# Attention outputs: their transposes ahead of a half run of values, their sums inverted by GpSimd

## The chip, the cores and the metric

One core of a Trainium2 chip runs the whole kernel. The metric is device time in microseconds (us) from launch to end, the median of several runs. The core's engines run in parallel, each in the order of its own queue, and wait for each other by semaphores: TensorE (PE in the profile, its weight loads PEld), VectorE (DVE), ScalarE (ACT), GpSimd (POOL), and SyncE (SP), which only issues transfers here. GpSimd issues transfers too.

## The reference

The kernel computes a conditioned transformer block on 2048 rows of 576 columns: layer norm and modulation, attention with 32 heads of 18 columns, then layer norm and a gated product. Only attention matters here; for each head it is

```python
H = 32; Dh = D // H            # D = 576, Dh = 18
scores = jnp.einsum("bhqd,bhkd->bhqk", q, k) * Dh ** -0.5
p = _softmax(scores, axis=-1)
o = jnp.einsum("bhqk,bhkd->bhqd", p, v)
x = x + ga * (o.transpose(0, 2, 1, 3).reshape(B, S, D) @ wo)
```

All data is in 32-bit floating point.

## The kernel before

**Units and steps.** Attention runs in 32 units (`u`): 16 pairs of heads (`p`) for the first 1024 query rows (`half` 0), then the same pairs for the other 1024. A unit has 16 steps (`kt`), one for each 128 keys. In a step TensorE makes four score tiles of 128 keys x 512 queries (L1055, two heads by two blocks of columns, each reading half of the array's rows), and ACT turns each into probabilities with one exponential (L1059). TensorE multiplies the probabilities of a step with the values two steps later (`values`, L629): four results side by side in one bank of PSUM, `o`, which gathers the sum over all 16 steps. A head's values have a 19th column of ones, so that row 18 of each head's result is the sum of the probabilities, by which the result has to be divided.

**Maxima.** The exponentials need each query's largest score. TensorE makes these scores ahead of time, for a later unit, with queries in rows (L524), and VectorE takes the maxima (L530, L535; for one tile in eight ACT helps with L533). The negated maxima of a unit are turned around (`spread`, L555) and stored as two more rows of the query operand.

**The order by hand.** In this stage the orders of TensorE and of ACT are written out; VectorE's and GpSimd's instructions are ordered by a planner when the kernel is built. A step's order is a string (L1028), one letter for each piece: `m` a score tile for maxima, `t` a score tile with its exponential, `v` a whole run of values (512 columns), `a` and `b` the two half runs (256 columns each) of another step's values, `k` the copy of a finished `o` (`taken`), `w` or `s` the place where outputs, `spread` and background work issue their first part, `c` where outputs and `spread` issue their second part.

There are two forms. The "halved" one has `vmmtmmtsactt` in even steps and `wmcmbkttmtmt` in odd ones. The other, for steps with much background work, has `vtmmttmvtm` and `ktmwttmctmm`. The form is chosen at each even step (L1021 to L1025), from step 10 on by

```python
hold = heavy and (kt == 2 or kt == 12 and u < UNITS - 1)
state["halved"] = step >= 10 and (hold or not heavy)
```

so steps 2 and 3 of every later unit are halved.

**Outputs.** When a unit's 16 runs of values are done, in step 1 of the next unit, ACT copies `o` to SBUF as `oT` (`taken`, L646). `outputs` (from L649) then has two parts. The first issues four transposes of 128x128 on TensorE (L656) into one PSUM bank, `tp`, which puts queries in rows. The second, at `c`, has VectorE take the reciprocal of the 16 sums per row from `tp` (L661, 128x16), ACT copy `tp` back over `oT` (L672, 128x512), and GpSimd multiply each head's 144 values with the reciprocals into the rows `Oa` or `big` (L676, two of 128x144). For the very last unit, both the reciprocal and the products are VectorE's (L665). In the kernel before, `outputs` is called in step 3 at `w`, so the transposes stand at the head of step 3, between two score tiles of step 2 and a tile for maxima.

**Banks.** Scores, maxima and transposes take turns in seven PSUM banks (`bank`, L89): each tile waits until the tile seven before it in this order has been read.

**Background work.** From unit 15 on, `first_rows` and `last_rows_project` project finished rows of outputs, one piece at a time, at the same letters: transposes L743 and L760, products L776, and in units 22 to 25 the transposes L886 of the normalized rows `z`, which GpSimd makes (L866). Earlier, `weigh` (L114) and `down_parts` (L912 on) use GpSimd to prepare weights of the next stage.

Of the kernel before, what the change touches and what calls it, by code (L numbers as in the profile page):

```python
# [15 lines left out]
F32 = mybir.dt.float32  # L16
F32R = mybir.dt.float32r
AF = mybir.ActivationFunctionType
ALU = mybir.AluOpType
# [4 lines left out]
P = 128  # L24
# [4 lines left out]
DH = 18  # L29
# [32 lines left out]
def tile_block(ctx, tc, x_in, wqkv, wo, w_gate, w_up, w_down, c_in, w_mod, out):  # L62
    nc = tc.nc
# [3 lines left out]
    const = ctx.enter_context(tc.tile_pool(name="const", bufs=1))  # L67
# [6 lines left out]
    make_identity(nc, ident)  # L74
    powers = const.tile([P, 8], F32, name="powers")
    nc.gpsimd.memset(powers, -0.5)
    mcol = const.tile([P, 2, 5], F32, name="mcol")
    mcol2 = const.tile([P, 2, 6], F32, name="mcol2")
    gb_b = const.tile([P, D], F32, name="gb_b")
    left = ExitStack()  # L80
# [8 lines left out]
    def bank():  # L89

        turns["bank"] += 1
        return ps[turns["bank"] % 7].tile([P, 512], F32, name=f"s{turns['bank'] % 7}")
# [458 lines left out]
    def spread(qs, nm):  # L551

        n = HW // P
        tp = bank()[0 : 2 * n, 0:P]
        nc.tensor.transpose(tp, nm.rearrange("p h t -> p (h t)"), ident)  # L555
        yield
        mrows = small.tile([32 + 2 * n, P], F32R, name="mrows", bufs=1)
        parts = [mrows[32 * l : 32 * l + 2 * n] for l in range(2)]
        nc.scalar.copy(parts[0], tp)
        nc.vector.tensor_sub(parts[1], tp, parts[0].bitcast(F32))  # L560
        for h in range(2):
            for l, part in enumerate(parts):
                to = 64 * h + 3 * DH + l
                nc.sync.dma_start(
                    qs[to : to + 1, :].rearrange("l (t q) -> l t q", q=P).bitcast(F32),
                    part[n * h : n * (h + 1), :].bitcast(F32),
                )
# [4 lines left out]
    def turn():  # L572
        if turns["s"] < turns["to"]:
            turns["s"] += 1
            next(todo, None)
# [37 lines left out]
    epool = att.enter_context(tc.tile_pool(name="epool", bufs=1))  # L613
# [6 lines left out]
    def values(cols=slice(0, 512)):  # L620

        half, p, kt, probs = pending[0]
        if kt == 0:
            state["o"] = po.tile([P, 512], F32, name="o")
        acc = state["o"]
        for h in range(2):
            for c in range(2):
                j = 2 * h + c
                nc.tensor.matmul(  # L629
                    acc[32 * j : 32 * j + 32, cols],  # L630
                    vaug[:, kt, (2 * p + h) * VW : (2 * p + h) * VW + 32],
                    probs[2 * c + h][:, cols],
                    start=kt == 0, stop=kt == NT - 1 and cols.stop == 512, tile_position=(0, 32 * j),
                )
        if cols.stop < 512:
            return
        pending.pop(0)
        if kt == NT - 1:
            state["whole"] = (half, p, acc)

    def taken():

        if "whole" in state:
            half, p, acc = state.pop("whole")
            oT = epool.tile([P, 512], F32, name="oT")
            nc.scalar.copy(oT, acc)  # L646
            state["end"] = (half, p, oT)

    def outputs():  # L649

        if "end" not in state:
            return
        half, p, oT = state.pop("end")
        tp = bank().rearrange("p (b q) -> p b q", q=P)
        for b in range(4):
            nc.tensor.transpose(tp[:, b, :], oT[:, b * P : (b + 1) * P], ident)  # L656

        yield
        tq = tp.rearrange("p b (j e) -> p j b e", e=32)
        rec = epool.tile([P, 4, 4], F32, name="rec")  # L660
        nc.vector.reciprocal(rec, tq[:, :, :, DH])  # L661
        if half == 1 and p == H // 2 - 1:
            state["last"] = epool.tile([P, 512], F32, name="oT")[:, 0 : 16 * DH].rearrange("p (t e) -> p t e", t=8)
            for h in range(2):
                nc.vector.tensor_tensor(  # L665
                    state["last"][:, :, h * DH : (h + 1) * DH].rearrange("p (c b) e -> p c b e", c=2),
                    tq[:, 2 * h : 2 * h + 2, :, 0:DH],
                    rec[:, 2 * h : 2 * h + 2, :].unsqueeze(3).to_broadcast([P, 2, 4, DH]),
                    op=ALU.mult,
                )  # L670
            return
        nc.scalar.copy(oT, tp.rearrange("p b q -> p (b q)"))  # L672
        tq = oT.rearrange("p (b j e) -> p j b e", j=4, e=32)
        for h in range(2):
            f0 = (2 * p + h) * DH
            nc.gpsimd.tensor_tensor(  # L676
                Os[half][:, :, f0 : f0 + DH].rearrange("p (c b) e -> p c b e", c=2),
                tq[:, 2 * h : 2 * h + 2, :, 0:DH],
                rec[:, 2 * h : 2 * h + 2, :].unsqueeze(3).to_broadcast([P, 2, 4, DH]),
                op=ALU.mult,  # L680
            )
# [328 lines left out]
    for u in range(UNITS):  # L1010
        half, p = divmod(u, H // 2)
# [5 lines left out]
        for kt in range(NT):  # L1017
# [11 lines left out]
            for does in order[kt % 2]:  # L1029
                if does == "m":  # L1030
                    turn()
                elif does == "k":
                    taken()
                elif does in "ws":
                    if kt == 3:
                        follow.append(outputs())
                        next(follow[-1], None)
                    if "spread" in state and halved == (does == "s"):
                        follow.append(spread(*state.pop("spread")))
                        next(follow[-1])  # L1040
                    if step >= FROM0 and not hold and halved == (does == "s"):
                        state["next"] = next(rows0 if step < FROM1 else rows1, None)
                elif does == "c":
                    while follow:
                        next(follow.pop(0), None)
                elif does == "v":
                    if step >= LAG:
                        values()
                elif does in "ab":
                    values(slice(0, 256) if does == "a" else slice(256, 512))  # L1050
                else:
                    c, h = next(sides)
                    sT = bank()
                    rows = slice(64 * h, 64 * h + 3 * DH + 2)
                    nc.tensor.matmul(  # L1055
                        sT, ks[rows, kcols], qs[rows, c * 512 : (c + 1) * 512], start=True, stop=True
                    )
                    pr = probs[2 * c + h] = ppool.tile([P, 512], F32, name=f"p{2 * c + h}")
                    state["exp"] = nc.scalar.activation(pr, sT, AF.Exp, scale=SCALE)  # L1059
            pending.append((half, p, kt, probs))  # L1060
            if u in (1, 3):
                if kt == 0:
                    a = big.tile([P, 8, 640], F32, name="big")
                    a = a.rearrange("p a b -> p (a b)")[:, 0 : 8 * D].rearrange("p (t c) -> p t c", t=4)
                    b = slots.tile([P, 2560], F32, name="w0")[:, 0 : 2 * D]
# [39 lines left out]
    for _ in outputs():  # L1105
        pass
# [13 lines left out]
    def region(name):  # L1120
        return ctx.enter_context(tc.tile_pool(name=name, bufs=1))
# [6 lines left out]
    sums = {1: region("sums"), 3: region("sums3")}  # L1128
# [456 lines left out]
    for n, (hf, b, k) in enumerate(seq):  # L1585
# [167 lines left out]
        if hf == 0 and b == NB - 1:  # L1753
# [3 lines left out]
            s = ORDER.index(k)  # L1757
# [31 lines left out]
```

## Time and profile before

| | us |
|---|---|
| runs shown (3): median | 2802.2 |
| lowest, highest | 2801.63, 2802.61 |
| span of the profiled execution, first to last instruction | 2801.3 |
| first and last L656 start | 280.5, 1536.0 |
| L656: 128 matmuls, median of one | 0.273 |
| L661: 32 reciprocals, median of one | 0.257 |
| L672: 31 copies by ACT, median of one | 0.736 |
| L676: 32 and 30 products by GpSimd, median of one | 0.432 and 0.430 |

The profiled execution's own time isn't given apart from its span; the median of the runs is 0.9 us above that span. TensorE's granted clock was 0.999 of full speed over the span.

In the timeline's rows the columns are: start, duration (of all instructions in the row, from the first start to the last end), engine, line, operation, tiles written and read, shape, and how many instructions the row merges. Square brackets give idle time of that engine before the row and what ended it. A weight load (PEld) marks the point at which TensorE takes up the matmul that belongs to it. In rows by line, the last columns are the total busy time in us, the mean of one in ns, and idle time before them in us.

### The profile page before, as it was taken

Reading aid. Unit: us, or ns where it says so; the run is one execution under the profiler, and the core shown is the slowest. Engines: PE = TensorE matmul, PEld = TensorE weight load, DVE = VectorE, ACT = ScalarE, POOL = GpSimd, SP = SyncE. Lnnn points to the kernel's source line nnn. Section 1 sums busy time; section 2 is a strip of 40 time slices with the busy share of each in tenths; the row PEclk is TensorE's granted clock in tenths of the full one; section 3 lists DMA queues with packets and bytes.
Section 4 is the critical chain, followed back from the end, with each engine's and each line's share of the span. In section 5 each row is a group of like instructions: output and inputs, shape, how many; then the busy total and the mean of one; then the engine's idle time right before and its main releaser. Section 6 shows DMA issues by size and latency. Waiting matters only on the chain.

```text
span 2801.3 us, 50850 instructions
## 1 busy us (share of the span) xinstructions
PE 2766.6 (99%) x18637; PEld 1830.4 (65%) x18637; DVE 2302.7 (82%) x4370; ACT 1607.0 (57%) x3051; POOL 816.2 (29%) x1077
## 2 busy tenths in 40 slices
PE   7999999999999999999999999999999999999999
PEld 5975444444444444444444888888888888888888
DVE  7278999999998888999883788888898677777777
ACT  3216999999999778999888322333333222222221
POOL 3125208887843111663113222222221100000000
PEclk9999999999999999999999999999999999999999
DMA  5344215444442120232126766667767966666663
GB/s 173 123 155 147 72 59 173 168 173 157 170 135 80 36 59 24 98 106 71 43 68 219 266 220 228 232 217 266 279 249 274 355 201 196 203 196 200 199 197 120
DMA packets 170778, 462.60 MB, mean 165 GB/s; under 512 B 21212, under 2 KB 88032, under 8 KB 160416
## 3 DMA queue, kind: packets, MB, share of 16 engines
q1 hardware_dynamic: 150064, 360.72, 38.7%
q0 software_dynamic: 20464, 98.62, 10.0%
q8 instruction: 147, 2.41, 0.4%
q14 instruction: 103, 0.84, 0.1%
HBM read 281.92 MB, written 176.82 MB: 164 GB/s over the span
## 4 chain that ended last, share of the span: by engine, by line
PE 93%; DVE 4%; issue 1%; DMA 1%; ACT 1%; POOL 0%; SPq 0%; DVEq 0%; ACTq 0%; POOLq 0%
PE x L1196 28%; PE o L629 19%; PE s L1055 12%; PE s L524 10%; PE d L1346 8%; PE d L1278 6%; PE s L310 4%; PE s L776 2%; PE s L363 1%; DVE mx L530 1%; PE s L656 1%; ACT p L1059 1%; DMA wq_raw<-in_A_wqkv_dram 0%; DVE Oa L1350 0%; DVE w L1186 0%
## 5 line engine op out<-in xcount | busy, mean ns | idle before, releaser
L1059 ACT ACTIVATE p<-s 128x512 f32<-128x512 f32 x2048 | 1078.1, 621 | 98.8 <-PE s L1055 83.5
L530 DVE TENSOR_REDUCE mx<-s 128x1 f32<-128x512 f32 x1568 | 993.8, 683 | 108.0 <-PE s L524 93.3
L629 PE MATMUL o<-p,vaug 128*32 128x256 f32 (+1 forms) x5848 | 592.4, 477 | 3.1 <-ACT p L1059 2.5
L1055 PE MATMUL s<-q,k 56*128 56x512 f32 x1920 | 516.6, 449 | 0.0
L524 PE MATMUL s<-k,q 54*128 54x512 f32 x1920 | 501.3, 427 | 2.6 <-DVE t L746 1.7
L524 PEld LDWEIGHTS s<-k,q 54*128 54x128 f32 x1920 | 275.6, 185 | 231.6 <-DVE mx L535 161.0
L1055 PEld LDWEIGHTS s<-q,k 56*128 56x128 f32 x1920 | 246.9, 184 | 242.7 <-issue 112.8
L1196 PE MATMUL x<-k,w 128*128 128x512 f32 x1512 | 368.6, 391 | 0.0
L1196 PEld LDWEIGHTS x<-k,w 128*128 128x128 f32 x1512 | 276.9, 188 | 53.1 <-issue 1.7
L629 PEld LDWEIGHTS o<-p,vaug 128*32 128x32 f32 x5848 | 115.4, 108 | 209.7 <-issue 130.7
L1346 PE MATMUL d<-wd,hh 128*128 128x288 f32 x1248 | 249.9, 295 | 2.4 <-DVE Oa L1350 2.4
L1196 PE MATMUL x<-big,w 128*128 128x512 f32 x1008 | 244.9, 391 | 2.1 <-DVE u L1690 1.4
L1196 PE MATMUL x<-w,w 128*128 128x512 f32 x1008 | 245.1, 391 | 0.0
L1196 PEld LDWEIGHTS x<-big,w 128*128 128x128 f32 x1008 | 185.1, 188 | 38.5 <-DVE u L1690 2.3
L1196 PEld LDWEIGHTS x<-w,w 128*128 128x128 f32 x1008 | 184.4, 188 | 34.3
L1346 PEld LDWEIGHTS d<-wd,hh 128*128 128x128 f32 x1248 | 202.2, 188 | 6.2 <-DVE Oa L1350 3.1
L1346 PE MATMUL d<-wd,hl 128*128 128x288 f32 x624 | 184.3, 295 | 0.0
L1350 DVE TENSOR_TENSOR Oa<-Oa,d 128x288 f32<-128x288 f32 x312 | 136.4, 452 | 54.8 <-PE d L1346 50.8
L535 DVE CUSTOM_DVE_ANT_0 over<-s,over 128x512 f32<-128x512 f32 x240 | 164.4, 685 | 0.7 <-ACT p L1059 0.3
L533 ACT ACTIVATE over<-s 128x512 f32<-128x512 f32 x240 | 150.1, 626 | 7.4 <-PE s L524 7.3
L1205 ACT ACTIVATE sg<-x 128x512 f32<-128x512 f32 x36 | 21.6, 599 | 207.8 <-PE x L1196 207.8
L1177 ACT CAST w<-S 128x768 fp32r<-128x768 f32 x71 | 59.4, 836 | 137.5 <-POOL S L1150 135.6
(274 smaller groups left out, 3889.8 us busy)
## 6 DMA issues: line engine op xcount, KB each, us to landing
ws<-w SPq DMA_DIRECT2D x126, 640.0 KB
w<-ws SPq DMA_DIRECT2D x126, 640.0 KB
wd<-wds SPq DMA_DIRECT2D x19, 1152.0 KB
k<-kd SPq DMA_DIRECT2D x60, 360.0 KB
wds<-w POOLq DMA_DIRECT2D x18, 1152.0 KB, 5.6
wtd<-t POOLq DMA_DIRECT2D x32, 576.0 KB, 4.8
wt<-wtd SPq DMA_DIRECT2D x64, 288.0 KB
wd<-wds SPq DMA_DIRECT2D x52, 288.0 KB
```

What stands on the lines that cost most here:

```text
L310: nc.tensor.matmul(acc, w, hT[:, t, cols], start=n == 0, stop=n == len(ts_) - 1)
L524: nc.tensor.matmul(sp, qs[rows, qt * P : (qt + 1) * P], ks[rows, at * 512 : (at + 1) * 512], start=True, stop=True,)
L530: nc.vector.tensor_reduce(to, sp, axis=AX.X, op=ALU.max)
L533: nc.scalar.activation(over, sp, AF.Relu)
L535: nc.vector.tensor_tensor_reduce(out=over, in0=sp, in1=over, scale=1.0, scalar=LOWEST, op0=ALU.add, op1=ALU.max, accum_out=mx[:, h * n + q ...
L629: nc.tensor.matmul(acc[32 * j : 32 * j + 32, cols], vaug[:, kt, (2 * p + h) * VW : (2 * p + h) * VW + 32], probs[2 * c + h][:, cols], star ...
L1055: nc.tensor.matmul(sT, ks[rows, kcols], qs[rows, c * 512 : (c + 1) * 512], start=True, stop=True)
L1059: state["exp"] = nc.scalar.activation(pr, sT, AF.Exp, scale=SCALE)
L1196: nc.tensor.matmul(acc[v], w[:, v, a, :], X[s][:, b, :], start=first and n == 0, stop=n == 6, skip_group_check=not first,)
L1278: nc.tensor.matmul(acc, a[:, rows], w[:, k, :], start=n == 0, stop=n == 2)
L1346: nc.tensor.matmul(acc[:, :HALF], a[:, f, rows], w[:, f, cols], start=n == 0, stop=n == 5)
L1350: nc.vector.tensor_add(Oa[:, t, cols], Oa[:, t, cols], acc[:, :HALF])
```

## The change

The call of `outputs` moves from step 3 at `w` to step 2 at `s`, which is directly ahead of the half run of values `a`; its second part then comes at the `c` of step 2, behind that half run and ahead of the last two score tiles of the step. Its reciprocal leaves VectorE (but for the last unit): GpSimd copies the 16 sums per row out of ACT's copy, raises them to the power -1 with a tile of constants, and improves the result with two rounds of `rec = rec * (2 - sums * rec)`. That is eight instructions of 128x16 on GpSimd for each output, ahead of its two products. The tile of constants is set once, at the start.

```diff
@@ -74,6 +74,8 @@
     make_identity(nc, ident)
     powers = const.tile([P, 8], F32, name="powers")
     nc.gpsimd.memset(powers, -0.5)
+    minus = const.tile([P, 16], F32, name="minus")
+    nc.gpsimd.memset(minus, -1.0)
@@ -658,8 +660,8 @@
         yield
         tq = tp.rearrange("p b (j e) -> p j b e", e=32)
         rec = epool.tile([P, 4, 4], F32, name="rec")
-        nc.vector.reciprocal(rec, tq[:, :, :, DH])
         if half == 1 and p == H // 2 - 1:
+            nc.vector.reciprocal(rec, tq[:, :, :, DH])
             state["last"] = epool.tile([P, 512], F32, name="oT")[:, 0 : 16 * DH].rearrange("p (t e) -> p t e", t=8)
@@ -671,6 +673,14 @@
             return
         nc.scalar.copy(oT, tp.rearrange("p b q -> p (b q)"))
         tq = oT.rearrange("p (b j e) -> p j b e", j=4, e=32)
+        sums = epool.tile([P, 4, 4], F32, name="sums")
+        left = epool.tile([P, 4, 4], F32, name="left")
+        nc.gpsimd.tensor_copy(sums, tq[:, :, :, DH])
+        nc.gpsimd.tensor_tensor(rec, sums, minus.rearrange("p (j b) -> p j b", b=4), op=ALU.pow)
+        for _ in range(2):
+            nc.gpsimd.tensor_mul(left, sums, rec)
+            nc.gpsimd.tensor_scalar(left, left, -1.0, 2.0, op0=ALU.mult, op1=ALU.add)
+            nc.gpsimd.tensor_mul(rec, rec, left)
@@ -1032,7 +1042,7 @@
                 elif does == "k":
                     taken()
                 elif does in "ws":
-                    if kt == 3:
+                    if kt == 2 and does == "s":
                         follow.append(outputs())
                         next(follow[-1], None)
```

## The prediction

> **What bounds the kernel now.** I read the page first: its span, the engines' busy shares and the chain that ended last.
>
> ```profile
> span 2801.3 us, 50850 instructions
> PE 2766.6 (99%) x18637; PEld 1830.4 (65%) x18637; DVE 2302.7 (82%) x4370; ACT 1607.0 (57%) x3051; POOL 816.2 (29%) x1077
> PE 93%; DVE 4%; issue 1%; DMA 1%; ACT 1%; POOL 0%; SPq 0%; DVEq 0%; ACTq 0%; POOLq 0%
> ```
>
> TensorE ends the work: 93% of the chain. Its busy time is modelled, so 99% doesn't say that it is full. The change touches attention alone, so next I read the timeline of TensorE's weight loads there, around one group of outputs' transposes (L656, called T below). "L629 x8" is a run of values; every two steps have one whole run and two half runs, A and B. Between them stand score matmuls (L1055) and maxima (L524) in pairs. I count the beat from one A to the next.
>
> ```profile
> 589.34 0.16 PEld L629 LDWEIGHTS o<-p,vaug 128*32 128x32 f32 x8 [0.30 <-ACT p L1059]
> 589.90 0.18 PEld L1055 LDWEIGHTS s<-q,k 56*128 56x128 f32 x2 [0.41 <-issue]
> 590.34 0.42 PEld L656 LDWEIGHTS s<-ident,oT 128*128 128x128 f32 x4 [0.25 <-ACT p L1059]
> 590.92 0.19 PEld L524 LDWEIGHTS s<-k,q 54*128 54x128 f32 x2 [0.17 <-ACT p L1059]
> 591.36 0.16 PEld L629 LDWEIGHTS o<-p,vaug 128*32 128x32 f32 x8 [0.25 <-issue]
> ...
> 594.73 0.16 PEld L629 LDWEIGHTS o<-p,vaug 128*32 128x32 f32 x8 [0.37 <-ACT p L1059]
> ...
> 599.36 0.16 PEld L629 LDWEIGHTS o<-p,vaug 128*32 128x32 f32 x8 [0.37 <-ACT p L1059]
> ...
> 608.73 0.16 PEld L629 LDWEIGHTS o<-p,vaug 128*32 128x32 f32 x8 [0.36 <-ACT p L1059]
> ```
>
> A starts at 589.34, 594.73 and 599.36, beats of 5.39 and 4.63 us; the two beats up to 608.73 take 9.37 together, so an ordinary one is 4.685 us: T lengthens its own, and the next gives 0.05 back. One T costs 5.39 + 4.63 - 2 x 4.685 = 0.65 us today. Its own four loads and their drain last 590.92 - 590.34 = 0.58; A to B is 2.02.
>
> Who sets the ordinary beat? In the brackets A waits for ACT's exponentials (0.30 us at 589.34). That is a ring: half runs and scores on TensorE, four exponentials on ACT, and the next A waits for the last of them. TensorE time between A and B lies in that ring, so time saved there counts, until ACT or a bank is late instead.
>
> **The change part by part.** (1) *T moves to just ahead of A.* Other transposes stand there already: L886, four of 128x128 as well, of the normalized rows.
>
> ```profile
> 1135.15 0.16 PEld L629 LDWEIGHTS o<-p,vaug 128*32 128x32 f32 x8 [0.17 <-issue]
> ...
> 1136.39 0.16 PEld L629 LDWEIGHTS o<-p,vaug 128*32 128x32 f32 x8 [0.37 <-issue]
> ...
> 1139.78 0.42 PEld L886 LDWEIGHTS s<-ident,z 128*128 128x128 f32 x4 [0.34 <-POOL z L866]
> 1140.37 0.16 PEld L629 LDWEIGHTS o<-p,vaug 128*32 128x32 f32 x8 [0.17 <-issue]
> ...
> 1145.00 0.42 PEld L886 LDWEIGHTS s<-ident,z 128*128 128x128 f32 x4 [0.34 <-issue]
> 1145.59 0.16 PEld L629 LDWEIGHTS o<-p,vaug 128*32 128x32 f32 x8 [0.17 <-issue]
> ...
> 1150.23 0.16 PEld L629 LDWEIGHTS o<-p,vaug 128*32 128x32 f32 x8 [0.35 <-ACT p L1059]
> ```
>
> From the load at 1139.78 to A at 1140.37 is 0.59 us: the same 0.58 as T costs itself. But A to B (1135.15 to 1136.39) is only 1.24, not 2.02. The beat 1140.37 to 1145.59 is 5.22, that is 4.63 without its 0.59; the beat after the last group is 4.64. So four transposes ahead of A cost 0.59 and give back 4.685 - 4.635 = 0.05: 0.54 net. Against today's 0.65, one T saves **0.11 us**.
>
> Bounds for this step: without the shorter beat behind it, 0.65 - 0.59 = 0.06. If TensorE's time between A and B alone decided, 2.02 - (1.24 + 0.58) = 0.20.
>
> In five units another group already stands ahead of that very A (L743 three times, L886 twice; first and last below), and T joins it. The only row of two groups joined is L555 with L886.
>
> ```profile
> 949.23 0.42 PEld L743 LDWEIGHTS s<-ident,Oa 128*128 128x128 f32 x4 [0.42 <-DVE mx L530]
> 949.82 0.16 PEld L629 LDWEIGHTS o<-p,vaug 128*32 128x32 f32 x8 [0.17 <-issue]
> 950.82 0.42 PEld L656 LDWEIGHTS s<-ident,oT 128*128 128x128 f32 x4 [0.24 <-issue]
> ...
> 955.21 0.14 PEld L760 LDWEIGHTS s<-ident,t 128*128 128x128 f32 x1 [0.37 <-issue]
> 955.48 0.16 PEld L629 LDWEIGHTS o<-p,vaug 128*32 128x32 f32 x8
> ...
> 1194.38 0.09 PEld L555 LDWEIGHTS s<-ident,nm 128*16 128x16 f32 x1 [0.34 <-ACT p L1059]
> 1194.82 0.42 PEld L886 LDWEIGHTS s<-ident,z 128*128 128x128 f32 x4 [0.36 <-issue]
> ...
> 1249.62 0.42 PEld L886 LDWEIGHTS s<-ident,z 128*128 128x128 f32 x4 [0.37 <-POOL z L866]
> ```
>
> The first of two joined groups takes 1194.82 - 1194.38 = 0.44. The beat 949.82 to 955.48 is 5.66, and 5.39 without the 0.27 of L760; the beat behind a group alone is 4.64, so T costs 0.75 there now. Joined it would cost 0.44: 0.31 saved (0.16 if 0.59 is paid all the same, 0.36 if only the loads of about 0.39 count).
>
> How many: ACT's copy behind T is issued 31 times. The last of them, in the last unit, has no maxima left to part from the scores and saves nothing: 25 plain ones and five joined. Sum: 25 x 0.11 + 5 x 0.31 = 2.75 + 1.55 = **4.3 us**. Bounds: 25 x 0.06 + 5 x 0.16 = 2.3, and 25 x 0.20 + 5 x 0.36 = 6.8.
>
> (2) *The wait of the moved T.* It needs oT, which ACT copies one step earlier. In the unit at 354.92 that copy is issued, and the A ahead of which T will stand is at 357.57: two us of room. T also needs a PSUM bank, freed by the last exponential of the step before, which A waits for anyway. Behind T in TensorE's queue stands that A, so a late T would move the whole ring.
>
> (3) *ACT's copy of T* (one before, one after) moves from behind the fourth exponential to between the second and the third. What hides it is ACT's idle time there.
>
> ```profile
> 354.92 0.63 ACT L646 COPY oT<-o 128x512 f32<-128x512 f32 x1
> 355.39 1.15 ACT L1059 ACTIVATE p<-s 128x512 f32<-128x512 f32 x2
> ...
> 357.57 0.16 PEld L629 LDWEIGHTS o<-p,vaug 128*32 128x32 f32 x8 [0.30 <-ACT p L1059]
> ...
> 591.10 0.26 DVE L661 RECIPROCAL rec<-s 128x16 f32<-128x16 f32 x1 [0.32 <-PE s L656]
> 591.47 0.75 ACT L672 COPY oT<-s 128x512 f32<-128x512 f32 x1
> ...
> 1139.96 1.13 ACT L1059 ACTIVATE p<-s 128x512 f32<-128x512 f32 x2
> 1141.53 3.30 ACT L1059 ACTIVATE p<-s 128x512 f32<-128x512 f32 x6 [0.44 <-PE s L1055]
> ...
> L672 ACT COPY oT<-s 128x512 f32<-128x512 f32 x31 | 21.1, 680 | 0.7 <-DVE rec L661 0.7
> ```
>
> A copy of this shape holds ACT for 0.47 (354.92 to 355.39). With T's stand-in at 1139.78, the second exponential starts near 1140.43, ACT is free for the next near 1140.90, and the third starts at 1141.53, when its scores are there. The copy fits into these 0.63 with 0.16 over, so I cost it at nothing. If it did not fit at all, it would cost 0.47.
>
> (4) *The reciprocal leaves VectorE*: 0.26 us, waiting for T. ACT's copy at 591.47 started behind it, but also just behind its fourth exponential. VectorE is not in the ring, and this doesn't move A: 0, at most its own 0.26 per output.
>
> (5) *GpSimd gets eight more instructions per output*, of 128x16.
>
> ```profile
> L197 POOL TENSOR_TENSOR r<-var,powers 128x4 f32<-128x4 f32 x6 | 6.6, 1106 | 44.9 <-DVE var L196 44.9
> L197 POOL TENSOR_TENSOR r<-var,powers 128x8 f32<-128x8 f32 x1 | 1.7, 1679 | 19.8 <-DVE var L196 19.8
> L676 POOL TENSOR_TENSOR Oa<-oT,rec 128x144 f32<-128x144 f32 x32 | 13.1, 433 | 94.9 <-ACT oT L672 94.7
> 1136.36 3.14 POOL L866 TENSOR_SCALAR z<-Oa,mv,rs 128x128 f32<-128x128 f32 x4
> 1505.26 0.60 SPq L1092 DMA_DIRECT2D oend<-big  x1
> 1525.22 3.90 SPq L1188 DMA_DIRECT2D ws<-w  x3
> ```
>
> The power took 1.11 us for 4 columns and 1.68 for 8, so about 0.14 a column: 2.8 for 16 as an estimate (1.1 if columns beyond four were free, and I find nothing to make it dearer than 3.4, twice the 8). The copy, four products and two scalings lie between 0.05 (0.43 by 16/144) and 0.43 each. That gives 1.4 to 6.4 us for the eight; with 0.2 for each of the seven, in the middle since a short instruction has its own fixed part, I take 4.2. The memset at the start is one more such, once. Over 31 outputs it is 130 us of an engine that is 29% busy. It hides if nobody needs GpSimd sooner. The nearest that does: z for the transposes at 1145.00 is made from 1136.36 to 1139.50, behind an output's products, with 5.5 us to spare; 4.2 fits. SP's queue waits for the last output's products before the store at 1505.26, and its next entry is at 1525.22, which has 20 us to spare. So 0. The next unit's copy into oT has to wait until GpSimd has read the last one: that is eight beats later, 37 us.
>
> The Trainium skill speaks against this part: "GPSIMD Engine Reference", section "Engine selection", gives elementwise work to VectorE and calls GpSimd about twice as slow for two inputs. The rows here are worse than that, 2.8 against 0.26, and the trace has VectorE idle for it. By that rule, with GpSimd on the path, the sum would be a loss; what bears it out or not stands in rival C.
>
> **The sum** against the profiled execution: 2801.3 - 4.3 = 2797.0 of span. The median of the runs shown, 2802.2, is 0.9 above that span, so the time is 2797.0 + 0.9 = **2797.9 us**.
>
> **The rivals.** *A: TensorE alone decides.* Then each change of the array's shape that disappears counts whole. A pair of scores is 0.44 long ahead of T (589.90 to 590.34) and one of maxima 0.44 behind it (590.92 to 591.36); put together they take 1.24 - 0.57 = 0.67. Saved: 6.8 us, 2795.4. For it: the chain is TensorE's. Against it: A's own wait of 0.30 for ACT. The Trainium skill has the rule in "TensorEngine Tiling (Array Packing)", "Key Properties": a change of tiling mode drains TensorE. The rows agree with that rule as far as the 0.2 us go.
>
> *B: ACT's copy stands in the way* (slower). If T's product is not there when the second exponential is done, ACT stands in order before the copy, and the third exponential, the bank it frees and the whole ring wait for up to 0.47 per output: 30 x 0.47 = 14.1 lost, 4.3 won, 2811.6 at full price. It decides from the point where T ends later than 1140.90 - 1139.78 = 1.12 us after it begins. Against it: A itself starts 0.59 after T does.
>
> *C: GpSimd is late.* If the eight take over 5.5 us, or stand ahead of z or of a split of rows in GpSimd's order, which the planner chooses, TensorE waits for the excess, 1 to 4 us at a few places: 2799 to 2804, no change or slightly slower. (With all of it on the path in every unit it would be 30 x (4.2 - 0.26) = 118 us, which I leave out: today's products by GpSimd stand in the same place and no row has TensorE wait for them.) Against it: 29% busy.
>
> *D: it doesn't come through*, the beat stays tied to the exponentials: at the lower bound, 2802.2 - 2.3 = 2799.9.
>
> **How the numbers follow.** About 0.2%, 5.6 us, is what a measurement here can tell from no change, so "faster" begins below 2796.6. The forecast has 0.50 (2795.5 to 2799), A 0.25, D 0.10, B 0.08, C 0.07. Faster: 0.20 from A and 0.10 from the forecast's lower end, 0.30. Slower: B and a tenth of the rest of C and surprises, 0.10. Same: 0.60. The range leaves out B's full price and the far end of A and C: 2793.5 to 2804.
>
> **What would show it.** Right: L656 directly ahead of an L629 half run, about 0.59 to it; A to B near 1.24; the beat with T ahead of A longer by 0.59 and the next near 4.64; no wait on ACT's copy that names T; L661 left once. Wrong: the beat behind T at 5 us or more with the third exponential late (B), or TensorE waiting at L886 or L776 for GpSimd (C). If the power takes well over 3.4 us, my GpSimd cost falls, though not the sum as long as nothing waits.

## The result: slower, and the profile after

The changed kernel takes 2834.2 us (median of 4 runs, 2831.28 to 2835.7) against 2802.4 for the kernel before beside it (2801.63 to 2806.96): ratio 1.0104, 95% interval 1.0089 to 1.0118. The forecast was 2797.9 with a range up to 2804. The page of the changed kernel: its span, busy times, and the chain that ended last.

```profile
span 2832.2 us, 51001 instructions
PE 2789.0 (98%) x18637; PEld 1834.2 (65%) x18637; DVE 2299.2 (81%) x4339; ACT 1608.5 (57%) x3051; POOL 952.2 (34%) x1326
PE 87%; POOL 4%; DVE 3%; DMA 2%; issue 2%; ACT 1%; SPq 0%; ACTq 0%; DVEq 0%; POOLq 0%
```

GpSimd, which had no share of the chain, now has 4% of it. To see where the 30.9 us of span come from, I compared the starts of ACT's exponentials step by step: 0.7 us arise before the first of them, 12.3 in attention, 17.9 behind it. Within attention, units 0, 13, 14 and 16 are 1.6, 0.9, 7.4 and 7.4 us longer, 17.3 together; the other 28 are 5.0 us shorter together. So there are three stories: a gain, stalls, and a slower last stage.

**The gain came.** TensorE's weight loads and ACT's rows of the changed kernel around one T, in the timeline (L658 is T, L631 values, L674 ACT's copy behind T):

```profile
585.96 0.16 PEld L631 LDWEIGHTS o<-p,vaug 128*32 128x32 f32 x8 [0.36 <-ACT p L1069]
...
590.74 0.42 PEld L658 LDWEIGHTS s<-ident,oT 128*128 128x128 f32 x4 [0.30 <-ACT p L1069]
590.96 1.20 ACT L1069 ACTIVATE p<-s 128x512 f32<-128x512 f32 x2
591.33 0.16 PEld L631 LDWEIGHTS o<-p,vaug 128*32 128x32 f32 x8 [0.17 <-issue]
591.91 0.73 ACT L674 COPY oT<-s 128x512 f32<-128x512 f32 x1
592.43 1.84 ACT L1069 ACTIVATE p<-s 128x512 f32<-128x512 f32 x3
592.57 0.16 PEld L631 LDWEIGHTS o<-p,vaug 128*32 128x32 f32 x8 [0.38 <-issue]
...
596.00 0.16 PEld L631 LDWEIGHTS o<-p,vaug 128*32 128x32 f32 x8 [0.37 <-ACT p L1069]
```

T to A is 591.33 - 590.74 = 0.59, A to B 1.24, the beat behind T 596.00 - 591.33 = 4.67. By these timelines the beat that ends in A grew from 4.79 to 5.37 us, and the one behind it shrank from 5.39 to 4.67: 0.58 paid, 0.72 won, 0.14 net. ACT's copy has no bracket: it waits for nobody.

**The stalls.** Rows of all engines from the same timeline: ACT's copy of T (L674), the start of GpSimd's chain on it (L678), its end (L686), and ACT's next copy into the one buffer `oT` (L648).

```profile
438.78 0.73 ACT L674 COPY oT<-s 128x512 f32<-128x512 f32 x1
444.19 0.22 POOL L678 COPY sums<-oT 128x16 f32<-128x16 f32 x1
...
615.30 0.21 POOL L678 COPY sums<-oT 128x16 f32<-128x16 f32 x1
...
626.36 0.62 ACT L648 COPY oT<-o 128x512 f32<-128x512 f32 x1
...
706.71 0.73 ACT L674 COPY oT<-s 128x512 f32<-128x512 f32 x1
736.29 0.21 POOL L678 COPY sums<-oT 128x16 f32<-128x16 f32 x1
741.40 0.82 POOL L686 TENSOR_TENSOR Oa<-oT,rec 128x144 f32<-128x144 f32 x2
742.25 0.59 ACT L648 COPY oT<-o 128x512 f32<-128x512 f32 x1 [0.92 <-POOL Oa L686]
746.09 0.67 ACT L674 COPY oT<-s 128x512 f32<-128x512 f32 x1
778.69 0.22 POOL L678 COPY sums<-oT 128x16 f32<-128x16 f32 x1
784.97 0.81 POOL L686 TENSOR_TENSOR Oa<-oT,rec 128x144 f32<-128x144 f32 x2
785.82 0.59 ACT L648 COPY oT<-o 128x512 f32<-128x512 f32 x1 [5.16 <-POOL Oa L686]
786.45 0.20 PEld L631 LDWEIGHTS o<-p,vaug 128*32 128x32 f32 x8 [5.56 <-ACT oT L648]
```

The chain starts 5.4 us behind its copy at 438.78, 23.4 behind the one at 591.91, 29.6 behind 706.71 and 32.6 behind 746.09. Some of that is old: in the kernel before, GpSimd takes up the products of the same four outputs 5.4, 9.2, 9.6 and 11.6 us behind the copy, the last one here:

```profile
745.17 0.75 ACT L672 COPY oT<-s 128x512 f32<-128x512 f32 x1
...
756.72 0.82 POOL L676 TENSOR_TENSOR Oa<-oT,rec 128x144 f32<-128x144 f32 x2
```

The next copy into `oT` is due 626.36 - 591.91 = 34.45 us after, and from the chain's start to the end of the products takes 5.9 and 7.1 us in the last two cases. So the chain is late first in unit 13 (0.92 us) and then in unit 14 (5.16), where TensorE stands for 5.56 us. The cause is seen in GpSimd's own time. The view by windows of the kernel before gives busy time (and instructions) of each engine in one unit, the granted clock, and the DMA share:

```profile
553.80:592.20 38.40, 38.40 (x327) 15.74 (x325) 35.39 (x68) 37.18 (x75) 32.69 (x53) 1.00 0.49 167
```

In this stage GpSimd was busy for 32.69 of 38.40 us, not 29%: it prepares weights in units 5 to 14. In the changed kernel the groups by line show what is added to that:

```profile
L679 POOL TENSOR_TENSOR rec<-sums,minus 128x16 f32<-128x16 f32 x31 | 90.9, 2931 | 2.1
L681 POOL TENSOR_TENSOR left<-sums,rec 128x16 f32<-128x16 f32 x62 | 13.8, 222 | 4.3
L682 POOL TENSOR_SCALAR left<-left 128x16 f32<-128x16 f32 x62 | 12.6, 204 | 5.1
```

With L678 and L683 that is 4.4 us an output, 37.1 of 38.4 together by this sum, and on top come GpSimd's waits for its own transfers. Over these units the queue falls behind, though not by the same amount in each. The end of the weights in both kernels' timelines, before first, shows by how much:

```profile
799.71 0.59 POOL L955 DMA_DIRECT2D wds<-w  x1 [0.30 <-POOL w L932]
816.72 0.55 POOL L698 DMA_DIRECT2D t<-in_A_wo_dram  x1 [16.41 <-DMA q<-qd]
```

```profile
829.24 0.66 POOL L965 DMA_DIRECT2D wds<-w  x1 [0.30 <-POOL w L942]
829.90 0.56 POOL L708 DMA_DIRECT2D t<-in_A_wo_dram  x1
...
886.64 0.29 POOL L766 COPY t<-Oa 128x128 f32<-128x128 f32 x1
...
886.99 0.14 PEld L770 LDWEIGHTS s<-ident,t 128*128 128x128 f32 x1 [4.55 <-POOL t L766]
```

Before, GpSimd was done at 799.71 and then waited 16.41 us for others; after, it ends at 829.24 and goes on without a pause. So the output weights and the chain of unit 16 come late too, and TensorE waits 4.55 us at L770 for the rows to project. The two long stalls have a tail. By the windows of the changed kernel the granted clock (the third column from the end) falls at the end of the stall in unit 14:

```profile
778.00:785.10 7.10, 3.21 (x30) 1.31 (x28) 4.30 (x8) 2.66 (x6) 6.57 (x12) 1.00 0.81 267
785.10:791.90 6.80, 5.44 (x26) 1.94 (x26) 1.89 (x3) 4.72 (x9) 6.70 (x12) 0.50 0.47 166
```

Of unit 14's 7.4 us, 5.3 are the step with the wait and 2.1 the two steps behind it, at half clock. The Trainium skill ("TensorE: Matmul & The Clock Gate", Part 1, "What's actually happening") says that an idle window of about 3.4 us halves TensorE's clock and a busy one restores it; the trace agrees: TensorE takes up nothing from 780.89 to 786.45, and the clock is half from 785.1 to 791.9.

**The last stage.** Its three largest groups, by line and form, before and after:

```profile
L1196 PE MATMUL x<-k,w 128*128 128x512 f32 x1512 | 368.6, 391 | 0.0
L1196 PE MATMUL x<-w,w 128*128 128x512 f32 x1008 | 245.1, 391 | 0.0
L1196 PE MATMUL x<-big,w 128*128 128x512 f32 x1008 | 244.9, 391 | 2.1 <-DVE u L1690 1.4 <-DVE u L1695 0.7
```

```profile
L1206 PE MATMUL x<-k,w 128*128 128x512 f32 x1512 | 376.4, 395 | 0.0
L1206 PE MATMUL x<-big,w 128*128 128x512 f32 x1008 | 250.1, 396 | 2.9 <-DVE u L1700 2.2 <-DVE u L1705 0.7
L1206 PE MATMUL x<-w,w 128*128 128x512 f32 x1008 | 249.8, 395 | 0.0
```

The same 3528 matmuls are busy 876.3 us instead of 858.6: 17.7 more, the whole excess of that stage. Nothing in it is touched by the change. What could differ is where its tiles lie: the constant `minus`, 64 bytes a partition, moves what is allocated after it. The run shift_only below tests that.

### The profile page after: what moved, and what is told of

The parts are those of the page before. It is cut to its first block, busy times and chain, and to the rows that moved or that the text cites. A ratio compares the mean times of both kernels' runs of the same rounds, so it can differ in the third digit from the quotient of the medians.

```text
span 2832.2 us, 51001 instructions
## 1 busy us (share of the span) xinstructions
PE 2789.0 (98%) x18637; PEld 1834.2 (65%) x18637; DVE 2299.2 (81%) x4339; ACT 1608.5 (57%) x3051; POOL 952.2 (34%) x1326
## 4 chain that ended last, share of the span: by engine, by line
PE 87%; POOL 4%; DVE 3%; DMA 2%; issue 2%; ACT 1%; SPq 0%; ACTq 0%; DVEq 0%; POOLq 0%
PE x L1206 28%; PE o L631 16%; PE s L1065 10%; PE s L526 9%; PE d L1356 8%; PE d L1288 6%; PE s L312 4%; PE s L786 2%; PE s L365 1%; ACT p L1069 1%; DVE mx L532 1%; POOL rec L679 1%; PE s L658 1%; DMA wq_raw<-in_A_wqkv_dram 1%; DMA t<-in_A_wo_dram 0%
## 5 line engine op out<-in xcount | busy, mean ns | idle before, releaser
L631 PE MATMUL o<-p,vaug 128*32 128x256 f32 (+1 forms) x5848 | 596.1, 479 | 8.9 <-ACT oT L648 6.7
L1206 PE MATMUL x<-k,w 128*128 128x512 f32 x1512 | 376.4, 395 | 0.0
L631 PEld LDWEIGHTS o<-p,vaug 128*32 128x32 f32 x5848 | 115.6, 108 | 213.5 <-issue 136.0
```

Source lines behind the costliest of these rows:

```text
L631: nc.tensor.matmul(acc[32 * j : 32 * j + 32, cols], vaug[:, kt, (2 * p + h) * VW : (2 * p + h) * VW + 32], probs[2 * c + h][:, cols], star ...
L1206: nc.tensor.matmul(acc[v], w[:, v, a, :], X[s][:, b, :], start=first and n == 0, stop=n == 6, skip_group_check=not first,)
```

## The experiments

Four theories stood at the start: **L**, GpSimd is late; **S**, the 64 bytes slow the last stage; and as rivals **M**, the moved transposes themselves cost, and **C**, another state of the chip. All ratios are against runs of the kernel before on the same chip. "Attention" and "last stage" are differences to the profile of before, from the first to the last exponential and from there to the end.

| run | median us | ratio, 95% interval | attention | last stage |
|---|---|---|---|---|
| changed kernel | 2834.2 | 1.0104, 1.0089 to 1.0118 | +12.3 | +17.9 |
| move_only | 2813.09 | 1.0027, 1.0016 to 1.0038 | +7.9 | +0.8 |
| gpsimd_only | 2837.64 | 1.0123, 1.0107 to 1.014 | +10.1 | +19.3 |
| shift_only | 2821.13 | 1.0057, 1.0042 to 1.0072 | +1.7 | +16.1 |
| two_oT | 2830.47 | 1.009, 1.0075 to 1.0105 | +9.3 | +16.9 |
| copy_first | 2799.71 | 0.998, 0.9971 to 0.999 | -5.4 | -0.2 |
| minus_freed | 2816.8 | 1.0043, 1.0029 to 1.0057 | +13.4 | +1.8 |
| second_half | 2802.28 | 0.9988, 0.9979 to 0.9997 | -5.1 | +0.1 |
| short_chain | 2805.95 | 0.9999, 0.999 to 1.0009 | +0.8 | -0.7 |
| pad_256 | 2805.26 | 1.0004, 0.9995 to 1.0013 | -0.1 | +2.3 |

**move_only**: the kernel before with only the new place of T.

```diff
-                    if kt == 3:
+                    if kt == 2 and does == "s":
```

> The kernel before with the transposes moved ahead of the half run A; the reciprocal stays on VectorE and reads PSUM. Theory L (the loss in attention comes from GpSimd's eight instructions, which its queue reaches up to a unit late): this kernel has none of them, so it should show the forecast of the move, 4 to 5 us below before, beats with A to B near 1.24, and no wait of ACT for GpSimd. Theory S (the 64 bytes of the tile of constants shift what is allocated after it, and that makes the last stage's 512-column matmuls slower): no tile here, so the last stage is as before, one such matmul every 227 to 230 ns. Rival M (the move itself upsets the order and costs): slower than before by 10 us or more.

It lost: 0.25 us in most ordinary units, and 8.2 us by the medians, where L expected a gain of 4 to 5 and M a loss of 10 or more. VectorE's and ACT's rows in its timeline tell why:

```profile
590.62 1.89 DVE L530 TENSOR_REDUCE mx<-s 128x1 f32<-128x512 f32 x3 [0.42 <-PE s L524]
592.43 0.25 DVE L661 RECIPROCAL rec<-s 128x16 f32<-128x16 f32 x1
592.77 0.59 ACT L672 COPY oT<-s 128x512 f32<-128x512 f32 x1 [0.29 <-DVE rec L661]
593.25 1.09 ACT L1059 ACTIVATE p<-s 128x512 f32<-128x512 f32 x2
```

At the new place the reciprocal stands behind three maxima in VectorE's queue, ACT's copy waits for it, and the third exponential waits behind the copy: 593.25 against 592.43 in the changed kernel, though T itself lies only 0.3 us later (591.06). The next A comes 5.06 us after this one (591.65 to 596.71), not 4.67. M holds in its direction, but for the pair of move and reciprocal; copy_first below separates the two.

**gpsimd_only**: the changed kernel with T back in step 3.

```diff
-                    if kt == 2 and does == "s":
+                    if kt == 3:
```

> The inversion on GpSimd and the tile of constants, with the transposes where they were. Theory L: waits of ACT's copy of the results for GpSimd's products in units 13 and 14 and of the transposes L770 or their like in unit 16, some 12 to 18 us in attention. Theory S: another 16 to 18 us in the last stage, 233 ns between 512-column matmuls. Together 28 to 36 us above before. Rival M: about as before.

Ordinary units differ from before by 0.03 us at most in the first twelve: at the old place it is worth nothing to take the reciprocal from VectorE. Units 14 and 16 stall, by 1.0 and 7.9 us: at 779.13 ACT's copy into `oT` stands 0.89 us for GpSimd's products. So the chain brings stalls without the move, as L says, though they are smaller in unit 14 and attention is 10.1 us longer where 12 to 18 were expected.

**shift_only**: the kernel before with the constant alone.

```diff
+    minus = const.tile([P, 16], F32, name="minus")
+    nc.gpsimd.memset(minus, -1.0)
```

> The kernel before with nothing but the tile of constants and its memset added; nobody reads it. Theory S: attention as before, the last stage at 233 ns per 512-column matmul, 14 to 18 us above before. Rival C (the slower matmuls of the last stage are a state of the chip or the trace of the clock's half-speed periods in attention, not of the addresses): the same as before within 1 us, 227 to 230 ns.

A constant that nobody reads costs 16.1 us in the last stage. S holds, and C falls, since runs of the kernel before on the same chip are not slower. Its first group by line equals the changed kernel's:

```profile
L1198 PE MATMUL x<-k,w 128*128 128x512 f32 x1512 | 376.5, 395 | 0.0
```

**two_oT**: the changed kernel with a second buffer for every other output of the first 26.

```diff
-            oT = epool.tile([P, 512], F32, name="oT")
+            two = p % 2 and 16 * half + p < 26
+            oT = (bgp if two else epool).tile([P, 512], F32, name="oT2" if two else "oT")
```

> The changed kernel with a second buffer for the copy of the results, used in turn by odd pairs of heads up to unit 25, so that ACT's next copy need not wait for GpSimd's products of the last one. Theory L: the two waits in units 13 and 14 (1.1 and 5.3 us in the changed kernel's trace, with the half-speed period behind them some 8.5 us together) go; the wait in unit 16, which is for the products themselves, stays: 7 to 9 us below the changed kernel, near 2826. If they are not what it cost: no change from 2834.

The stalls of units 13 and 14 are gone, which shows that they hung on the one buffer. But unit 16 now loses 14.6 us instead of 7.4: GpSimd ends that unit's products at 883.80, only 2.8 us sooner than in the changed kernel, and the wait has passed on to the next who needs it. So the run is 3.7 us below the changed kernel, not the 7 to 9 expected.

From here the question was what each part is worth without the others.

**copy_first**: T at its new place, VectorE's reciprocal kept, but behind ACT's copy and from SBUF.

```diff
-        nc.vector.reciprocal(rec, tq[:, :, :, DH])
         if half == 1 and p == H // 2 - 1:
+            nc.vector.reciprocal(rec, tq[:, :, :, DH])
...
         tq = oT.rearrange("p (b j e) -> p j b e", j=4, e=32)
+        nc.vector.reciprocal(rec, tq[:, :, :, DH])
...
-                    if kt == 3:
+                    if kt == 2 and does == "s":
```

> The kernel before with the transposes moved one step earlier, as the change has them, and VectorE's reciprocal kept, but taken from ScalarE's copy in SBUF and behind it, so that the copy waits for nobody; no GpSimd chain, no constant. Theory of the copy's place (the move alone lost 0.25 us a unit because the copy stood behind a reciprocal that stood behind three maxima): the unit is 0.14 to 0.16 us shorter, as in the changed kernel, the third and fourth exponentials wait for nothing new, the last stage is as before: about 4.5 us faster than before, ratio 0.9984. Rival (VectorE's queue): VectorE, which takes its work in order, now stands at the reciprocal until the copy is done, the maxima and differences behind it come later by up to 0.7 us a unit, and the time is that of the move alone again, ratio 1.002 to 1.003.

It beats both kernels: 0.998. Its rows for VectorE and ACT, to be held against those of move_only:

```profile
587.58 1.89 DVE L530 TENSOR_REDUCE mx<-s 128x1 f32<-128x512 f32 x3 [0.41 <-PE s L524]
589.17 0.74 ACT L672 COPY oT<-s 128x512 f32<-128x512 f32 x1
589.71 1.83 ACT L1060 ACTIVATE p<-s 128x512 f32<-128x512 f32 x3
590.01 0.25 DVE L674 RECIPROCAL rec<-oT 128x16 f32<-128x16 f32 x1 [0.55 <-ACT oT L672]
```

The copy waits for nobody. VectorE does stand for 0.55 us, as the rival said, but loses nothing by it: ordinary units are 0.15 us shorter, as in the changed kernel.

**minus_freed**: the changed kernel, its constant in the pool that attention gives back.

```diff
-    minus = const.tile([P, 16], F32, name="minus")
-    nc.gpsimd.memset(minus, -1.0)
...
+    minus = epool.tile([P, 16], F32, name="minus")
+    nc.gpsimd.memset(minus, -1.0)
```

> The changed kernel with the 64 bytes of the constant laid into the attention's pool, which is given back ahead of the last stage, so that the last stage's tiles lie where they lay before. Theory of the shift: the 512-column matmuls of the last stage go back from 233.9 ns start to start to 228.8, the time behind the last exponential is within 1.5 us of before's instead of 17.9 above it, and the late GpSimd's 12 us in attention stay: ratio 1.004 to 1.005 against before. Rival (the last stage is slower for another reason that the change brings, such as GpSimd's share of the memory or the stalls behind it): the last stage stays 16 to 18 us longer, ratio 1.010.

The last stage is back within 1.8 us of before's (1.5 was expected; its matmuls start every 228.8 ns again), and the stalls stay (7.0 and 5.8 us in units 14 and 16; units 0 and 20 are 3.0 and 2.4 us longer in this profile, each with a period of half clock). Against the changed kernel's ratio the shift is worth 0.0061, about 17 us.

**second_half**: as minus_freed, with GpSimd's chain only where it prepares no weights.

```diff
+        if half == 0:
+            nc.vector.reciprocal(rec, tq[:, :, :, DH])
+        else:
...
```

> The changed kernel with the constant in the attention's pool, and with GpSimd's chain for the outputs of the second half alone, while those of the first half, in which GpSimd prepares weights, have VectorE's reciprocal from ScalarE's copy. Theory of the late GpSimd: the stalls of the changed kernel in units 13, 14 and 16 (13 us together) are gone, the second half's units are 0.15 us shorter as there, and the last stage is as before: ratio 0.998 to 0.9985, no slower than with VectorE in both halves. Rival (the chain itself costs, wherever it stands): the second half's units are no shorter than before's, or units 16 and 17 stall by 5 us or more; ratio 1.001 or above.

No stall is left, and the second half's units are as short as with VectorE there. So no cost of the eight instructions is seen where GpSimd prepares no weights: L holds. GpSimd is busy again in units 22 to 25, and an output's products start up to 18.2 us behind its copy there, but the next copy is due only some 35 us after, and nobody waits. The ratio is a little above the 0.998 to 0.9985 expected; whether the run is as fast as copy_first is not settled (0.9988 and 0.998, the intervals overlap).

**short_chain**: as minus_freed, without the two rounds of refinement.

```diff
-        for _ in range(2):
-            nc.gpsimd.tensor_mul(left, sums, rec)
-            nc.gpsimd.tensor_scalar(left, left, -1.0, 2.0, op0=ALU.mult, op1=ALU.add)
-            nc.gpsimd.tensor_mul(rec, rec, left)
```

> The changed kernel with the constant in the attention's pool and without the two rounds that refine GpSimd's reciprocal (six of its eight instructions ahead of the products, 1.3 of some 4.4 us); the reciprocal's accuracy is that of the power alone. Theory of the late GpSimd (the chain waits in GpSimd's queue behind the preparation of weights and its transfers): units 14 and 16, 7.0 and 5.8 us longer with the whole chain, stay at least 5 and 4 us longer; ratio 1.003 to 1.004 against before. Rival (the chain's own length decides): both lose in the same share as the chain or more, to 4 us and less; ratio below 1.002.

Half a miss: the ratio is the rival's, 0.9999 where 1.003 to 1.004 was expected. Unit 16 stays 6.1 us longer, but unit 14's stall, expected to stay, is gone. In its timeline the products that had been late now end just ahead of ACT's copy:

```profile
775.34 0.82 POOL L681 TENSOR_TENSOR Oa<-oT,rec 128x144 f32<-128x144 f32 x2
777.85 0.62 ACT L648 COPY oT<-o 128x512 f32<-128x512 f32 x1
```

They end at 776.16, with 1.7 us to spare. Some 1.3 us less an output, over ten units, is enough to stay inside the 34 us. It is a threshold: length matters through what it adds up to, not in proportion. The planner might also have given the chain a later place in GpSimd's order, but the traces speak against it. Ahead of the products of the output that made unit 14 wait, GpSimd ran 528 instructions other than those of outputs in the kernel before, and 529 in the changed kernel and in short_chain, one more by the constant's memset. So the place is the same there, and the queue in front takes longer. (For two earlier outputs the changed kernel's place is six or seven instructions later.) In unit 16 pace is not all. There GpSimd also waits for the last transfer of the output weights, longer than in the kernel before; their timelines, before first:

```profile
855.86 1.42 POOL L709 TENSOR_TENSOR t<-t,ga_b 128x576 f32<-128x576 f32 x1 [3.83 <-DMA t<-in_A_wo_dram]
```

```profile
865.69 1.42 POOL L714 TENSOR_TENSOR t<-t,ga_b 128x576 f32<-128x576 f32 x1 [9.57 <-DMA t<-in_A_wo_dram]
```

Why that transfer takes longer wasn't looked into.

**pad_32, pad_128, pad_192, pad_256**: shift_only with other sizes.

```diff
+    minus = const.tile([P, 64], F32, name="minus")
+    nc.gpsimd.memset(minus, -1.0)
```

(64 is pad_256; the others have 8, 32 and 48.)

> The kernel before with a constant of 32 bytes a partition and its memset alone. Moving the later tiles by 64 bytes took the last stage's 512-column matmuls from 228.8 to 233.9 ns, by 256 bytes to 228.8 again. If the place within 64 bytes counts too, 32 gives a pitch of its own, above 230 ns; if only whole steps of 64 count, or a tile begins at a multiple of 64 anyway, 228.8 or 233.9.

> The same with 128 bytes. If the place within 256 bytes counts, the pitch differs from 228.8 ns, between it and 233.9 or above; if the place within 128 bytes counts, it is 228.8, as with 256.

> The same with 192 bytes. If the place within 128 bytes counts, the pitch is that of 64 bytes, 233.9 ns; if the place within 256 counts, it may be any.

> The kernel before with a constant of 256 bytes a partition and its memset on GpSimd, and nothing else: as the run with the shift of 64 bytes alone, but four times as far. If what counts is where a tile lies within a stretch of 256 bytes or less (theory of the alignment), the last stage is as before, 228.8 ns a matmul, ratio 1.000. If any other place makes the matmuls slower (rival: the place against something that doesn't move along), it is 10 to 20 us longer as with 64 bytes, ratio 1.005. A wider alignment can give any pitch between 226.9 and 233.9 ns.

| bytes a partition | 0 | 32 | 64 | 128 | 192 | 256 |
|---|---|---|---|---|---|---|
| start to start of the 512-column matmuls, mean ns | 228.8 | 233.8 | 233.8 | 232.7 | 231.8 | 228.8 |
| last stage against before, us | 0 | +17.0 | +16.1 | +12.3 | +9.5 | +2.3 |

(The mean is over all such pairs less than 400 ns apart.) The pitch at 256 bytes is that of no shift to the last digit shown, and 64 and 192 differ, so these runs fit a rule by the place within a stretch of 256 bytes. Each has a memset on GpSimd, that of 256 bytes too, so the memset is not what costs. With 32 bytes the pitch is that of 64, so they don't tell whether a smaller step than 64 counts. The 2.3 us at 256, like the 1.8 of minus_freed, are not the pitch. pad_256's first group by line is the kernel before's:

```profile
L1198 PE MATMUL x<-k,w 128*128 128x512 f32 x1512 | 368.6, 391 | 0.0
```

The pads of 32, 128 and 192 had one timed run each (2821.14, 2817.62 and 2815.13 us beside 2805.04); their pitch is read from the trace.

## Why the prediction was wrong

**Step (1), the move: right in place and size, with the reciprocal gone.** 0.14 to 0.16 us in most ordinary units, where 0.11 was forecast; T to A 0.59 and A to B 1.24 as read off the other transposes. Among the joined units, 22 and 25 gave 0.45 and 0.42 (forecast 0.31, upper bound 0.36), 18 to 20 only 0.16 to 0.19, about the lower bound. Units 2 and 4 gave nothing; unit 17, counted as a plain one, gave 0.38, and the last unit, costed at nothing, 0.41. Why these differ was not looked into. Together 5.0 us where 4.3 was forecast.

**Steps (3) and (4): each right, but not independent.** The copy fits between the exponentials, and the reciprocal's leaving is worth nothing at the old place (gpsimd_only). At the new place it decides: with a reciprocal ahead of the copy the unit is 0.25 longer, without it 0.15 shorter, a swing of 0.40 us. That is the forecast's rival B by another hand. (B's full price is 2802.2 + 14.1 - 4.3 = 2812.0 by its own numbers, not 2811.6; nothing hangs on it.) The copy's source was in time, but its turn hung on VectorE. The change takes the reciprocal out of the way as a side effect; copy_first does so by order alone. So the gain, which was forecast for the move by itself, came in part by luck.

**Step (5) failed: "Over 31 outputs it is 130 us of an engine that is 29% busy. It hides if nobody needs GpSimd sooner."** The size was right, 4.2 forecast and 4.4 measured. The 29% is a mean over the span; in a unit in which GpSimd prepares weights it was 85%, and ten outputs fall there. The profile of before had the sign: products that start 11.6 us behind their copy at 745.17. And the deadline was wrong: "eight beats later, 37 us" was compared with the length of one chain, not with the queue in front of it. The deadline itself measured 34.45. The chain started up to 32.6 us behind its copy, and the same buffer that the prediction named made ACT, and then TensorE, wait. Rival C named a late GpSimd, but at z and the projections only and at 1 to 4 us; units 13, 14 and 16 lost 15.8, half clock included; the 7.4 of unit 16 are at the projections, the rest at `oT`, which C left out. minus_freed and second_half show this term by itself: 1.0043 with the chain in both halves, 0.9988 with it in the second alone. The page of the Trainium skill that the prediction weighed against this step ("GPSIMD Engine Reference", "Engine selection") points to the right sign: copy_first, with the reciprocal on VectorE, is below the kernel before. But it speaks of one instruction's speed, and the losses here came by a queue and by an address.

**A term was missing.** Costing the constant as "one more such, once" took only its memset into account. Its 64 bytes cost 16 to 18 us, more than all the rest (shift_only, minus_freed).

**What stays open.** Why the pitch depends on the address was not tried further, nor whose address it is, the weights' or the moved operand's. Unit 0's 1.6 us don't follow the change: shift_only has them too (1.5), move_only doesn't, and the trace gives a period of half clock there; what sets it off is unknown.

## What to carry to other kernels

Ask of an engine that is to get more work how full it is in the very stretch where the work falls, and count what stands ahead in its queue against the next use of the buffer. When work moves earlier, look at what each follower waits for at the new place: a copy behind another engine's short instruction also waits for what stands ahead of that instruction in its queue. And a new constant ahead of large tiles is a change of its own: put it where it is given back, or compare the groups of the stages that weren't touched.

## What the runs showed of the hardware

The 512-column matmuls of the last stage, whose weight loads last 188 ns with or without the shift, start every 228.8 ns in the kernel before and every 233.9 in the changed one, by how far an unread constant shifts what is allocated after it: 2% of the pitch, with a period that fits 256 bytes. GpSimd takes 0.20 to 0.22 us for a product, scaling or copy of 128x16, and 2.93 for a power of the same shape.
